# An mLSTM layer with a channel-mixing FFN: products with the old state summed in the bank of those within the chunk, PSUM as three rings, weight decoding without a clamp, and a new list

## The chip, the cores and the metric

The program runs on one core of one Trainium2 chip. TensorE (PE), VectorE (DVE), ScalarE (ACT) and GpSimd (POOL) each work through their own queue in the order in which the program was written for them; SyncE (SP) issues the transfers. The metric is device microseconds of one execution, as the median of several.

## The reference

Four batches of eight heads go through 768 steps of an mLSTM cell with a head size of 40; the result, seen as tokens of 320 numbers, goes through a channel-mixing feed-forward layer (FFN).

```python
for t in range(S):
    m_new = np.maximum(f_gate[:, :, t] + m, i_gate[:, :, t])
    f_stab = np.exp(f_gate[:, :, t] + m - m_new)
    i_stab = np.exp(i_gate[:, :, t] - m_new)
    m = m_new
    C = f_stab * C + i_stab * outer(vt, kt)
    n = f_stab * n + i_stab * kt
    h_tilde = C @ qt
    denom = np.maximum(np.abs(n @ qt), 1.0)
    y[:, :, t] = sigmoid(o_gate[:, :, t]) * h_tilde / denom
...
xk = mu_k * x + (1.0 - mu_k) * x_prev
xr = mu_r * x + (1.0 - mu_r) * x_prev
k = np.maximum(xk @ w_k, 0.0)
v = k * k @ w_v
r = sigmoid(xr @ w_r)
out = r * v
```

## The kernel before

The 768 steps are cut into six chunks of 128, and a **unit** is one chunk of two batches (NB = 2): units 0 and 1 are chunk 0 of batches 0, 1 and 2, 3, units 2 and 3 are chunk 1, and so on to unit 11. Each piece of work is a small function named with its unit `u` and the batch `i` within it; the body of the program is a list of calls of these functions, written out by hand (`load_w("wk", 0, SY)`, `ffn_k(0, 0)`, ...), and each engine gets its instructions in the order of that list. Nothing reorders them later.

*Attention of a unit.* `fetch_m` broadcasts the row of stabilisers of a batch to all partitions (tile `e`), `mask` (POOL) writes -1e30 where the key comes after the query, `exps` (ACT, eight of 128x128) makes the decay weights in place. In chunk 0 there is no row in DRAM yet: there `spread` makes it on PE, by eight products with a column of the identity (tile `pM`, K = 32), and `mask` clears the wrong half after `exps`. `scores` makes eight products of keys and queries (`pS`, two banks), `weigh` (DVE) multiplies them into `e`. `attend` does three things on PE: `e` times the values (`pI`, 16 products), the queries times the old state `C` (`pX`, eight), and the chunk's own addition to the state (`pX`, eight). In chunk 0 the second part is absent. `inter_v` (L306, DVE) scales the second part by the queries' decay `gk`, `total` (L314, DVE) adds the first, and `norm`, `gate`, `outcome`, `twin` make the layer's output `x`, which `turn` (PE) and `turned` (ACT) transpose. `carry_in` makes the scaled keys `kt`, `carry_old` the decayed state `Cd`, `carry_add` the new state.

*FFN of a unit.* `change` and `mix` (DVE, L373) make the mixed inputs, `mix_h` and `mix_l` (L388) split them in a high and a low part, so that PE can multiply in its fast format: `ffn_k` (L452, 16 products of 256 columns, four calls a unit, `pk`), `relu`, `square`, `square_h`, `square_l` (L479), `ffn_v` (L508, six products of 320 columns in a call, eight calls a unit, `pv`), `ffn_r` (L486, `pr`), `logits`, `sigmoid`, `result`, `store`.

*Weights.* They come as 64-bit floats, whose words the core turns into 32-bit floats, piece by piece: eight pieces of `wk` (384 wide), three of `wr` and eight of `wv` (320 wide). For each, `load_w` fetches, `size` (ACT, absolute value of the high word), `guard` (DVE, L413, a maximum with a smallest number), `bits` 0 to 2 (DVE, L420, L422, L424, shifts and masks), `parts` (the high part, mostly ACT) and `parts_l` (L436, the low part). This goes on beside units 0 and 1, so DVE has a great deal to do at the start.

*PSUM.* Eight banks: two for `pk` and the second `pr`, two for `pS`, two shared by `pI`, `pX` and the second `pv`, one for transposes and one for the first `pv` and the first `pr`.

*Fillers.* `warm(n)` issues n products of 512 columns of ones on PE (tile `pW`, L96), 58 in all, between the products of units 0 and 1.

What the prediction speaks of: `ffn_k(1, ·)`, the FFN of unit 1, before which PE has the whole of the start; `mix_l(0, "k")` and `mix_l(1, "k")`, the last DVE steps before `ffn_k(0, ·)` and `ffn_k(1, ·)`.

Of the kernel before, what the change touches and what calls it, by code (L numbers as in the profile page):

```python
# [18 lines left out]
P = 128  # L19
# [20 lines left out]
def mlstm_cmix_kernel(ctx: ExitStack, tc, kq, vk, og, gi, gf, wk, wr, wv, mu, pad, out):  # L40
# [8 lines left out]
    def bank(tag, name):  # L49
        return ps.tile([P, 512], F32, tag=tag, name=name, bufs=2 if tag in "kSA" else 1)  # L50
# [52 lines left out]
    gk = cp.tile([P, CPB, 2, BH], F32, name="gk")  # L103
# [106 lines left out]
    def mask(u, i):  # L210
# [55 lines left out]
    def attend(u, i):  # L266
# [3 lines left out]
        pI = t["I", i] = bank("A", "pI")  # L270
        pX = t["X", i] = bank("A", "pX") if cc else pI
        t["hv", i] = pI[:, :H * E1].rearrange("p (h x) -> p h x", x=E1)
        for h in range(H):
            at = slice(h * E1, (h + 1) * E1)
            for r in (slice(0, 64), slice(64, 128)):
                T.matmul(pI[r, at], t["e", i][:, h, r], t["va"][:, i, at], start=True, stop=True)  # L276
        if cc:
            for p in range(HH):
                at = slice(p * 2 * E1, (p + 1) * 2 * E1)
                for j in range(2):  # L280
                    s = i * L + 64 * j
                    T.matmul(pX[64 * j:64 * j + 64, at], kq_sb[u % 2][:KX, 1, p, s:s + 64], C[b][:KX, p, :],  # L282
                             start=True, stop=True)
        if cc < CPB - 1:
            for p in range(HH):
                for j in range(2):
                    h = p + HH * j
                    T.matmul(pX[64 * j:64 * j + D, H * E1 + p * E1:H * E1 + (p + 1) * E1], t["kt", i][:, h, :],  # L288
                             t["va"][:, i, h * E1:(h + 1) * E1], start=True, stop=True)

    def carry_add(u, i):
# [3 lines left out]
        pC = t["X", i][:, H * E1:H * E1 + HH * E1].rearrange("p (h x) -> p h x", x=E1)  # L295
# [6 lines left out]

    def inter_v(u, i):
        t, _, cc, _, bh = where(u, i)
        t1 = t["t1", i] = p2.tile([P, H, E1], F32, name="t1")
        V.tensor_tensor(t1.rearrange("p (j h) x -> p h j x", j=2),  # L306
                        t["X", i][:, :H * E1].rearrange("p (h j x) -> p h j x", j=2, x=E1),
                        gk[:, cc, 0, bh].rearrange("p (j h) -> p h j", j=2).unsqueeze(3)
                        .broadcast_to([P, HH, 2, E1]), op=ALU.mult)

    def total(u, i):
        t = units[u]
        t1 = t["t1", i]
        V.tensor_tensor(t1, t["hv", i], t1, op=ALU.add)  # L314
        t["hv", i] = t1
# [30 lines left out]
    def turn(u, i):  # L346
# [3 lines left out]
        pT = t["T", i] = bank(BANK["T"], "pT")  # L350
# [54 lines left out]
    def size(nm, i):  # L405
        p = pieces[nm, i]
        wf = p["wf"] = p2.tile([P, p["w"]], F32, tag="wf", name="wf", bufs=3)
        A.activation(wf, p["hi"].bitcast(F32), AF.Abs)

    def guard(nm, i):  # L410

        wf = pieces[nm, i]["wf"]
        V.tensor_scalar(wf, wf, SMALL, None, op0=ALU.max)  # L413

    def bits(nm, i, step):
# [3 lines left out]
        if step == 0:  # L419
            V.tensor_scalar(wb, wb, 3, 0x3FFFFFFF, op0=ALU.logical_shift_left, op1=ALU.bitwise_and)  # L420
# [1453 lines left out]
```

## Time and profile before

| | |
|---|---|
| median of 3 runs | 339.14 us (338.86 to 339.79) |
| span of the profiled execution | 336.5 us |
| its own time | not listed apart; the median of the runs lies 2.6 us above the span |
| PE busy | 321.8 us (96%) |
| DVE / ACT / POOL busy | 265.8 / 220.5 / 133.3 us |
| DMA | 41.99 MB |

The span goes from the first to the last instruction; the time has what lies around it too. Busy times of PE are modelled per product, so that they show where PE had something to do, not how fast. In the profile a product in full 32-bit format is recorded as two, so that eight calls of `scores` read x16.

### The profile page before, as it was taken

The page shows a single profiled execution, that of the slowest core. Times are in us where ns is not written, and L with a number is a line of the kernel's source. Part 1 is how long each engine was busy: PE and PEld are TensorE (multiplying, and loading weights), DVE is VectorE, ACT ScalarE, POOL GpSimd, SP SyncE. Part 2 cuts the span into 40 slices and gives each one's busy share as a digit, 9 for nine tenths or more (in the row PEclk, how much of TensorE's full clock was granted, in tenths as well). Part 3 has the DMA queues.
Part 4 walks back from the last instruction along what each step waited for, and adds up shares of the span by engine and source line. Part 5 has one row for each costly group of instructions (what it writes and reads, how often), then busy time and mean ns, then how long its engine had stood idle before and what let it go on. Part 6 is the DMA issues. An engine that isn't in the chain of part 4 may idle for free.

```text
span 336.5 us, 8857 instructions
## 1 busy us (share of the span) xinstructions
PE 321.8 (96%) x3544; PEld 296.7 (88%) x3548; DVE 265.8 (79%) x585; ACT 220.5 (66%) x484; POOL 133.3 (40%) x159
## 2 busy tenths in 40 slices
PE   8998895999999999999999999999999999999996
PEld 5576593999989999999999899999999899998995
DVE  6889999999999897767786976998596747778241
ACT  3577983689666768658828838839758655935350
POOL 2132234505333644455316435364524356353131
PEclk9979999699999999999999999999999999999999
DMA  6749644474523931612634641624214540010011
GB/s 207 248 144 288 177 171 160 126 215 152 152 103 97 285 106 34 209 64 86 157 98 131 215 124 51 228 84 143 59 64 109 193 163 0 5 58 2 0 42 39
DMA packets 14322, 41.99 MB, mean 125 GB/s; under 512 B 1912, under 2 KB 5144, under 8 KB 13320
## 3 DMA queue, kind: packets, MB, share of 16 engines
q1 hardware_dynamic: 14280, 41.41, 40.0%
q8 instruction: 28, 0.46, 0.6%
q14 instruction: 14, 0.11, 0.1%
HBM read 37.39 MB, written 4.01 MB: 123 GB/s over the span
## 4 chain that ended last, share of the span: by engine, by line
PE 70%; DVE 18%; ACT 6%; DMA 3%; issue 2%; POOL 0%; SPq 0%; ACTq 0%; POOLq 0%
PE pv L508 20%; PE pk L452 20%; PE pI L276 6%; PE pS L246 6%; PE pr L486 5%; PE pW L96 3%; PE pX L282 3%; PE pM L224 3%; ACT e L235 2%; DMA kq<-kq 2%; DVE e L251 2%; PE pT L352 2%; DVE kh L474 2%; DVE xm L373 1%; PE pX L288 1%
## 5 line engine op out<-in xcount | busy, mean ns | idle before, releaser
L452 PE MATMUL pk<-xlk,wkh 128*128 128x256 f32 x288 | 75.7, 279 | 0.0
L508 PE MATMUL pv<-wvh,kh 128*128 128x320 f32 x192 | 61.2, 319 | 0.2 <-DVE t L314 0.2
L508 PE MATMUL pv<-wvh,kl 128*128 128x320 f32 x192 | 59.3, 309 | 0.8 <-DVE kl L479 0.8
L508 PE MATMUL pv<-wvl,kh 128*128 128x320 f32 x192 | 59.2, 308 | 0.0
L458 ACT ACTIVATE rl<-pk 128x512 f32<-128x512 f32 x48 | 28.1, 590 | 42.4 <-PE pk L452 42.3
L452 PE MATMUL pk<-xhk,wkh 128*128 128x256 f32 x192 | 55.2, 287 | 0.0
L452 PEld LDWEIGHTS pk<-xlk,wkh 128*128 128x128 f32 x288 | 54.3, 188 | 0.0
L452 PE MATMUL pk<-xhk,wkl 128*128 128x256 f32 x192 | 53.5, 279 | 0.0
L235 ACT ACTIVATE e<-e,acol 128x128 f32<-128x128 f32 x160 | 50.0, 390 | 0.1
L214 POOL TENSOR_SCALAR_AFFINE_SELECT e<-e 128x1024 f32<-128x1024 f32 x24 | 28.0, 1166 | 47.0 <-DMA e<-nm 24.3
L479 POOL TENSOR_TENSOR kl<-kk,kh 128x512 fp32r<-128x512 f32 x20 | 28.7, 1436 | 39.4 <-DVE kh L474 25.7
L373 DVE SCALAR_TENSOR_TENSOR xm<-xd,mu_sb,xT 128x256 f32<-128x256 f32 x72 | 36.9, 567 | 3.1 <-POOL xd L367 3.0
L474 DVE CAST kh<-kk 128x512 fp32r<-128x512 f32 x44 | 24.4, 560 | 17.0 <-ACT kk L464 16.8
L452 PEld LDWEIGHTS pk<-xhk,wkh 128*128 128x128 f32 x192 | 36.2, 188 | 1.4 <-ACT rl L458 0.2
L508 PEld LDWEIGHTS pv<-wvh,kh 128*128 128x128 f32 x192 | 36.2, 188 | 1.0 <-issue 0.5
L508 PEld LDWEIGHTS pv<-wvh,kl 128*128 128x128 f32 x192 | 36.0, 188 | 1.0 <-DVE kl L479 1.0
L452 PEld LDWEIGHTS pk<-xhk,wkl 128*128 128x128 f32 x192 | 36.2, 189 | 0.0
L508 PEld LDWEIGHTS pv<-wvl,kh 128*128 128x128 f32 x192 | 36.1, 188 | 0.0
L251 DVE TENSOR_TENSOR e<-pS,e 128x512 f32<-128x512 f32 x48 | 32.1, 681 | 3.7 <-PE pS L246 3.2
L246 PE MATMUL pS<-kq 40*128 40x128 f32 x384 | 30.4, 293 | 1.0 <-DMA kq<-kq 1.0
L464 ACT ACTIVATE kk<-rl 128x512 f32<-128x512 f32 x48 | 29.5, 624 | 1.6 <-POOL kl L479 0.9
L276 PEld LDWEIGHTS pI<-vk_sb,e 128*64 128x64 f32 x768 | 24.8, 140 | 6.0 <-DVE e L251 1.9
(116 smaller groups left out, 724.6 us busy)
## 6 DMA issues: line engine op xcount, KB each, us to landing
e<-nm SPq DMA_DIRECT2D x20, 512.0 KB
vk_sb<-vk SPq DMA_DIRECT2D x12, 648.0 KB
kq<-kq SPq DMA_DIRECT2D x24, 320.0 KB
sg<-og SPq DMA_DIRECT2D x12, 320.0 KB
out<-sg SPq DMA_DIRECT2D x24, 160.0 KB
wst<-wk SPq DMA_DIRECT2D x8, 384.0 KB
wst<-wv SPq DMA_DIRECT2D x8, 320.0 KB
wst<-wr SPq DMA_DIRECT2D x3, 320.0 KB
```

The costliest lines, as they stand in the source:

```text
L214: G.affine_select(e, e, pattern=[[0, H], [1, L]], compare_op=ALU.is_ge, fill=NEG if cc else 0.0, base=0, channel_multiplier=-1)
L235: A.activation(e[:, h, :], src, AF.Exp, bias=acol[:, cc, b * H + h:b * H + h + 1])
L246: T.matmul(pS[j][:, p * L:(p + 1) * L], kq2[rw, 0, p, cs], kq2[rw, 1, p, cs], start=True, stop=True)
L251: V.tensor_tensor(ev, t["S", i, half], ev, op=ALU.mult)
L276: T.matmul(pI[r, at], t["e", i][:, h, r], t["va"][:, i, at], start=True, stop=True)
L373: V.scalar_tensor_tensor(xm[:, ct, :].rearrange("p (b t) -> p b t", b=NB), t["xd"][:, ct], mu_sb[:, "kr".index(nm), ct:ct + 1], xT[u % G2] ...
L452: T.matmul(pk[:, i * U:(i + 1) * U], ww[:, 2 * pr + i, ct * P:(ct + 1) * P], xx[:, ct, :], start=n == 0, stop=n == len(tl) - 1)
L458: A.activation(r, t["pk", pr], AF.Relu)
L464: A.activation(kk, t["r", pr], AF.Square)
L474: eng.tensor_copy(kh, t["kk", pr])
L479: eng.tensor_tensor(kl, t["kk", pr], t["kh", pr].bitcast(F32), op=ALU.subtract)
L508: T.matmul(t["pv", i][:, :DM], xx[:, ts], ww[:, f, :], start=f == 0 and n == 0, stop=f == NF - 1 and n == 2)
```

## The change

Four things change together.

1. The queries are scaled by their decay before the product with the old state. `gain` (ACT) makes exp of a whole row of 128 steps for all 32 heads and SP stores it in DRAM (`eg`, five times); `fetch_g` brings it back for each batch, broadcast over 64 partitions (two transfers, 64 x 4 x 128 each), and `queries` (DVE, 104x512) multiplies the queries into it. The product of these with the old state is then summed by PE in the same bank as `pI`. `inter_v` and `total` go, `pX` goes, and `columns` transposes two rows in place of three.
2. In chunk 0 the mask comes from PE: one product of 512 columns in each of `spread`'s eight banks (identity times a matrix of 0 and -1e30), on which the others are added. The four `mask` calls of chunk 0 go. Heads of a pair are neighbours now (2p and 2p + 1), so `exps` and `weigh` take every other head.
3. PSUM becomes three rings: two banks for `pI` and transposes, four for `pM`, `pS`, `pk` and `pr`, two for `pv`.
4. Weights are decoded without `guard`: `size` scales by a power of two, so `bits` 0 is one shift. The list of calls is made anew, with 12 fillers in place of 58. Ten `outcome`, ten `square_l` and three `mix_l` move from POOL to DVE, five `parts_l` of `wk` from DVE to POOL.

```diff
-SMALL = struct.unpack("<f", struct.pack("<I", (1023 - 127) << 20))[0]
-BANK = {"g": "T", "T": "T", ("r", 0): "v", ("r", 1): "k", ("v", 0): "v", ("v", 1): "A"}
+TO_SINGLE = 2.0 ** -112
+BANK = {"g": "A", "T": "A", "M": "B", "S": "B", "I": "A", "k": "B", ("r", 0): "B", ("r", 1): "B", ("v", 0): "v", ("v", 1): "v", "W": "v"}
+BANKS = {"A": 2, "B": 4, "v": 2}
...
+    def gain(c, eng):
+        eg = p2.tile([BH, L], F32, name="eg")
+        A.activation(eg, rows[c]["ar"][:, 1, :], AF.Exp)
+        eng.dma_start(eg_dram[c], eg)
...
     def spread(u, i):
...
+            T.matmul(pM, ident_b, later.unsqueeze(1).broadcast_to([P, HH, L]), start=True, stop=False)
...
+    def fetch_g(u, i, eng):
+        t, b, cc, _, bh = where(u, i)
+        t["g", i] = p2.tile([P, HH, L], F32, name="g")
+        rows_g = eg_dram[cc][bh, :].rearrange("(p j) t -> j p t", j=2)
+        for j in range(2):
+            eng.dma_start(t["g", i][64 * j:64 * j + 64], rows_g[j].partition_broadcast(64))
+
+    def queries(u, i, eng):
+        t, _, _, cs, _ = where(u, i)
+        q = t["g", i][:KX]
+        eng.tensor_tensor(q, kq_sb[u % 2][:KX, 1, :, cs], q, op=ALU.mult)
...
     def attend(u, i):
-        pI = t["I", i] = bank("A", "pI")
-        pX = t["X", i] = bank("A", "pX") if cc else pI
+        pI = t["I", i] = bank("I", "pI")
...
+                    mms.append((pI[r, at], t["g", i][:KX, p, r], C[b][:KX, p, :]))
...
+        for n, m in enumerate(mms):
+            T.matmul(*m, start=n < 2, stop=n >= len(mms) - 2, skip_group_check=True)
...
-    def inter_v(u, i):
...
-    def total(u, i):
...
     def size(nm, i):
-        A.activation(wf, p["hi"].bitcast(F32), AF.Abs)
-
-    def guard(nm, i):
-        wf = pieces[nm, i]["wf"]
-        V.tensor_scalar(wf, wf, SMALL, None, op0=ALU.max)
+        A.activation(wf, p["hi"].bitcast(F32), AF.Abs, scale=TO_SINGLE)
...
-            V.tensor_scalar(wb, wb, 3, 0x3FFFFFFF, op0=ALU.logical_shift_left, op1=ALU.bitwise_and)
+            V.tensor_scalar(wb, wb, 3, None, op0=ALU.logical_shift_left)
```

On PE, at the first attention (unit 0, both batches), the rows stood like this before: `attend(0, 0)`, `spread(1, 1)`, `attend(0, 1)`, fillers.

```order
L276 MATMUL pI<-vk_sb,e 64x41 x16
L288 MATMUL pI<-vk_sb,kt 40x41 x8
L224 MATMUL pM<-ar,ident 128x128 x8
L276 MATMUL pI<-vk_sb,e 64x41 x16
L288 MATMUL pI<-vk_sb,kt 40x41 x8
L96 LDWEIGHTS fill
L96 MATMUL pW<-fill 128x512
```

After the change the same place reads so (`scores(0, 1)`, `spread(1, 0)` with its two mask products, `attend(0, 0)`, `attend(0, 1)`):

```order
L268 MATMUL pS<-kq_75 128x128 x8
L229 LDWEIGHTS ident_b
L229 MATMUL pM<-later,ident_b 128x512
L232 MATMUL pM<-ar,ident 128x128 x4
L229 LDWEIGHTS ident_b
L229 MATMUL pM<-later,ident_b 128x512
L232 MATMUL pM<-ar,ident 128x128 x4
L313 MATMUL pI<-vk_sb,e 64x41 x16
L313 MATMUL pI<-vk_sb,kt 40x41 x8
L313 MATMUL pI<-vk_sb,e 64x41 x16
L313 MATMUL pI<-vk_sb,kt 40x41 x8
```

No filler stands between the fourth filler at the very start and the eight ahead of `ffn_k(0, 0)` any more, and the two `attend` follow each other.

On DVE, around the low part of unit 1's mixed input (`xlk`, which `ffn_k(1, ·)` waits for), the rows before were these; pieces of `wv` (tiles `wst`, `wf`, `wvl`) are decoded after it.

```order
L388 TENSOR_TENSOR xlk<-xm,xhk 128x768
L115 SCALAR_TENSOR_TENSOR bm<-ones,gf_sb 32x128
L424 SCALAR_TENSOR_TENSOR wf<-wst,wf 128x320
L123 SCALAR_TENSOR_TENSOR bm<-gf_sb,bm 32x128
L413 TENSOR_SCALAR wf<-wf 128x320
L422 SCALAR_TENSOR_TENSOR wf<-wst,wf 128x320
```

After the change the last piece of `wv` is decoded ahead of `xlk`:

```order
L425 TENSOR_SCALAR wf<-wf 128x320
L427 SCALAR_TENSOR_TENSOR wf<-wst,wf 128x320
L429 SCALAR_TENSOR_TENSOR wf<-wst,wf 128x320
L377 TENSOR_TENSOR xd<-xT_82 128x3x128 x2
L383 SCALAR_TENSOR_TENSOR xm<-xd,mu_sb,xT_82 128x256 x3
L273 TENSOR_TENSOR e<-pS,e 128x4x128
L441 TENSOR_TENSOR wvl<-wf,wvh 128x320
L398 TENSOR_TENSOR xlk<-xm,xhk 128x768
```

So all weights are decoded before the FFN of unit 1 begins, and PE does all eight `ffn_v(0, ·)` and `attend(2, 0)` ahead of `ffn_k(1, ·)`, where before it did them later. That last `attend` shows what else moved on PE; before, its second and third part went to a bank of their own:

```order
L276 MATMUL pI<-vk_sb,e 64x41 x16
L282 MATMUL pX<-C_75,kq_73 64x82 x8
L288 MATMUL pX<-vk_sb,kt 40x41 x8
```

After, all three go to one bank, and the second reads the scaled queries `g`:

```order
L313 MATMUL pI<-vk_sb,e 64x41 x16
L313 MATMUL pI<-C_77,g 64x82 x8
L313 MATMUL pI<-vk_sb,kt 40x41 x8
```

The number and shape of these products are the same.

## Rows read from the trace of the kernel before

**Rows 1.** The page: busy time, share of the span, instructions.

```profile
PE 321.8 (96%) x3544; PEld 296.7 (88%) x3548; DVE 265.8 (79%) x585; ACT 220.5 (66%) x484; POOL 133.3 (40%) x159
```

**Rows 2.** Windows: stretch, its length, busy PE, PEld, DVE, ACT, POOL, clock, DMA share, GB/s.

```profile
0.00:5.40 5.40, 3.88 (x12) 1.39 (x12) 2.60 (x9) 1.69 (x2) 1.83 (x12) 1.00 0.60 193
20.90:24.30 3.40, 3.40 (x32) 1.79 (x28) 3.40 (x8) 2.00 (x6) 0.38 (x1) 0.52 0.25 60
24.30:44.30 20.00, 17.09 (x276) 12.66 (x276) 19.24 (x53) 16.46 (x36) 5.42 (x8) 1.00 0.74 219
58.40:65.30 6.90, 6.89 (x32) 5.97 (x32) 6.90 (x13) 4.76 (x10) 4.40 (x4) 0.52 0.58 178
65.30:333.30 268.00, 264.79 (x3043) 255.47 (x3041) 206.20 (x445) 177.40 (x382) 111.98 (x127) 1.00 0.36 108
```

**Rows 3.** Timeline of PE, 0 to 66 us: start, length, line, products, idle before.

```profile
1.52 3.59 PE L96 MATMUL pW<-fill 128*128 128x512 bf16 x8 [1.52 <-DVE fill L70]
5.05 0.52 PE L156 MATMUL pt_g<-ident,ar 32*128 32x32 f32 x3
5.39 3.76 PE L224 MATMUL pM<-ar,ident 32*128 32x128 f32 x16
9.08 5.72 PE L96 MATMUL pW<-fill 128*128 128x512 bf16 x14
14.73 2.04 PE L224 MATMUL pM<-ar,ident 32*128 32x128 f32 x16
39.39 1.04 PE L96 MATMUL pW<-fill 128*128 128x512 bf16 x4
56.91 0.74 PE L352 MATMUL pT<-ident,x 128*128 128x128 f32 x3 [3.59 <-DVE x L340]
58.44 2.75 PE L246 MATMUL pS<-kq 40*128 40x128 f32 x16
65.87 0.28 PE L452 MATMUL pk<-xhk,wkh 128*128 128x256 f32 x1
```

**Rows 4.** Timeline of DVE, 0 to 80 us.

```profile
41.68 1.34 DVE L388 TENSOR_TENSOR xlk<-xm,xhk 128x768 fp32r<-128x768 f32 x1
66.27 0.29 DVE L413 TENSOR_SCALAR wf<-wf 128x320 f32<-128x320 f32 x1
77.95 0.49 DVE L436 TENSOR_TENSOR wvl<-wf,wvh 128x320 fp32r<-128x320 f32 x1
```

**Rows 5.** The chain that ended last, 104 to 116 us: start, length, work.

```profile
104.59 1.06 PE pI L276 x32
105.65 0.59 PE pX L282 x16
106.25 0.31 PE pX L288 x16
106.55 1.09 PE pS L246 x16
114.19 0.88 PE pv L508 x6
```

**Rows 6.** Groups by line and form: busy, mean ns of one, idle before.

```profile
L413 DVE TENSOR_SCALAR wf<-wf 128x384 f32<-128x384 f32 x8 | 3.3, 419 | 0.5 <-ACT wf L408 0.5
L413 DVE TENSOR_SCALAR wf<-wf 128x320 f32<-128x320 f32 x11 | 3.4, 312 | 0.0
L420 DVE TENSOR_SCALAR wf<-wf 128x320 int32<-128x320 int32 x11 | 6.6, 611 | 0.0
L306 DVE TENSOR_TENSOR t<-pX,gk 128x328 f32<-128x328 f32 x20 | 9.9, 496 | 17.0 <-PE pX L288 9.7 <-PE pX L282 7.3
L314 DVE TENSOR_TENSOR t<-pI,t 128x328 f32<-128x328 f32 x20 | 9.9, 493 | 0.3
L479 DVE TENSOR_TENSOR kl<-kk,kh 128x512 fp32r<-128x512 f32 x28 | 23.0, 822 | 0.3
```

**Rows 7.** The chain that ended last, 0 to 70 us: one transfer.

```profile
30.79 5.66 DMA kq<-kq
```

More of the change, by code (lines that the diff above doesn't have):

```diff
@@ L808, in mlstm_cmix_kernel @@
[L808 to L830 removed]
+    bits("wk", 7, 2)
@@ new lines, in mlstm_cmix_kernel @@
+    gate_o(5, SY)
+    mask(5, 1)
+    exps(5, 1, 1)
+    relu(3, 2)
+    norm(4, 1, 0)
+    norm(4, 1, 1)
+    norm(4, 1, 2)
+    gate(4, 1, V)
+    outcome(4, 1, V)
+    square(3, 2, A)
+    square_h(3, 2, V)
+    relu(3, 3)
+    scores(5, 0)
+    exps(5, 0, 1)
+    weigh(5, 0, 1)
+    turned(4, 0)
+    queries(5, 0, V)
+    exps(5, 1, 0)
+    scores(5, 1)
+    twin(4, 1, G)
+    square(3, 3, A)
+    square_h(3, 3, V)
+    turn(4, 1)
+    change(4, 0, V)
+    ffn_v(3, 1, 0, 1)
+    ffn_v(3, 1, 1, 2)
@@ new lines, in mlstm_cmix_kernel @@
+    carry_in(6, 0, V)
+    norm(5, 1, 0)
+    norm(5, 1, 1)
+    norm(5, 1, 2)
+    gate(5, 1, V)
+    outcome(5, 1, V)
+    carry_in(6, 1, G)
+    relu(4, 0)
+    square(4, 0, A)
+    square_h(4, 0, V)
+    fetch_g(6, 0, SY)
+    change(5, 0, V)
+    square(4, 1, A)
+    square_l(4, 0, V)
+    twin(5, 1, V)
+    square_h(4, 1, V)
+    square_l(4, 1, V)
+    ffn_k(4, 2)
+    relu(4, 2)
+    ffn_k(4, 3)
+    turn(5, 1)
+    exps(6, 0, 1)
+    ffn_v(4, 1, 0, 1)
+    ffn_v(4, 1, 1, 2)
+    load_o(6, SY)
@@ L1294, in mlstm_cmix_kernel @@
-    mix_l(5, "r", G)
-    norm(6, 0, 0)
-    norm(6, 1, 2)
-    load_o(7, SY)
-    norm(6, 0, 1)
-    columns(4)
-    relu(5, 3)
+    ffn_v(4, 0, 2, 3)
+    ffn_k(5, 1)
+    exps(6, 1, 1)
+    weigh(6, 1, 1)
+    sigmoid(4)
+    gate(6, 0, V)
+    attend(6, 1)
+    outcome(6, 0, V)
+    twin(6, 0, V)
+    carry_add(6, 0)
+    store(3, 0, SY)
+    scores(7, 0)
+    norm(6, 1, 0)
+    norm(6, 1, 1)
+    norm(6, 1, 2)
+    load_s(8, SY)
+    mix_h(5, "r")
+    square_l(4, 3, V)
+    relu(5, 0)
+    mix_l(5, "r", G)
@@ L1365, in mlstm_cmix_kernel @@
     norm(7, 0, 2)
+    square(6, 2, A)
+    gate(7, 0, V)
+    outcome(7, 0, V)
+    fetch_m(8, 1, SY)
+    mask(8, 1)
+    fetch_g(8, 0, SY)
+    ffn_v(5, 0, 2, 3)
+    mix_h(6, "r")
+    queries(8, 0, V)
+    ffn_v(5, 1, 3, 4)
+    result(5, 1)
+    ffn_k(6, 1)
+    relu(6, 1)
+    carry_in(7, 1, V)
+    twin(7, 0, V)
+    mix_l(6, "r", V)
+    turn(7, 0)
+    turned(7, 0)
+    store(4, 0, SY)
+    square_h(6, 2, V)
+    square_l(6, 2, G)
+    fetch_g(7, 1, SY)
+    queries(7, 1, V)
+    ffn_k(6, 0)
@@ new lines, in mlstm_cmix_kernel @@
+    sigmoid(6)
+    norm(8, 0, 2)
+    gate(8, 0, V)
+    queries(8, 1, V)
+    ffn_v(6, 0, 3, 4)
+    fetch_g(9, 1, SY)
+    queries(9, 1, V)
+    mix_h(7, "k")
+    carry_old(8, 1, V)
+    outcome(8, 0, V)
+    ffn_v(6, 1, 3, 4)
+    attend(8, 1)
+    carry_in(9, 0, G)
+    carry_old(8, 0, V)
+    fetch_m(9, 1, SY)
+    store(5, 1, SY)
+    mix_h(7, "r")
+    fetch_g(9, 0, SY)
+    carry_add(8, 0)
+    exps(9, 0, 0)
+    weigh(9, 0, 0)
+    carry_add(8, 1)
+    mix_l(7, "k", G)
+    ffn_k(7, 1)
```

2175 lines of the change are left out of this document (1007 added, 1168 removed).

## The prediction

> **What bounds the kernel now.** The page comes first: PE is busy for 321.8 of 336.5 us [rows 1], so it seems to bind throughout. That share is an average over two stages, and a table of windows parts them. From 65.3 to 333.3 us PE is idle for 268.0 - 264.8 = 3.2 us [rows 2]: there only PE counts. Before that its busy time says little, because fillers stand in it; the timeline of PE shows them in between the real products, and a gap of 3.59 us in front of one transpose, released by DVE [rows 3]. In the same stage DVE is busy for 19.24 of 20.0 us (24.3 to 44.3) and for all of 58.4 to 65.3 [rows 2]: it decodes weights. So the kernel is a start that ends with the first product of `ffn_k(1, ·)` at 65.87 [rows 3], set by DVE with PE and ACT in a chain, and a long stage set by PE. The question for each edit is which of the two it touches.
>
> The third thing is the clock. The windows show 0.52 from 20.9 to 24.3 and from 58.4 to 65.3 [rows 2]: the lower level, 1.2 of 2.4 GHz. They show 1.00 for 0 to 5.4, yet a filler takes 3.59 / 8 = 449 ns there and 5.72 / 14 = 409 ns from 9.08 on, against 1.04 / 4 = 260 ns at 39.39; `spread` takes 3.76 us at 5.39 and 2.04 at 14.73 [rows 3]. I therefore read the first 14 us as the lower level too, whatever that column says: lengths of equal work are the better witness. What PE did before 20.9 was `spread` and `scores`, narrow products of 32 and 40 rows; before 58.4 it had stood idle for 3.59 us.
>
> **The change part by part.**
>
> *The two DVE operations on the old state.* `inter_v` and `total` cost 9.9 + 9.9 us in 20 instructions each; `queries` adds 20 of 104x512. The nearest row is `square_l` on DVE, also two SBUF inputs and 512 columns, at 822 ns: 16.4 us, and below it the two removed ones, about 500 ns for 328 columns, give 20 x 0.50 = 10 us [rows 6]. With ten `square_l`, ten `outcome` and three `mix_l` more, DVE ends up with more work, not less. All but a first one or two lie after 65.9, beside a PE with 3.2 us of idle [rows 2]. If they wait on nothing late this is worth between -3.2 us (all of PE's idle recovered) and about +1.5 (a new stall in unit 1, where DVE barely keeps up); I take 0. The products keep number and shape; the new bank moves them without changing their 1.06 + 0.59 + 0.31 us [rows 5].
>
> The Trainium skill, "SBUF — State Buffer", section "Who interferes with whom", says that a DVE instruction with two SBUF inputs contends with a GpSimd one that reads SBUF; `queries` is such a one where `total` read PSUM. By that rule `queries` would lie at the dear end. The row agrees so far that `square_l` takes 822 ns where a 328-wide operation takes 493.
>
> *`guard`.* 19 instructions, 3.3 + 3.4 = 6.7 us of DVE [rows 6], all before 78.4. This one does lie in the start, where DVE sets the time; it is inside the counts below.
>
> *The start, step by step.* The gate transposes end and `spread` begins at 5.4 as now [rows 3]. The new list has four fillers, then `spread`, `spread`, `scores`, `columns`, `scores`, `spread`, `attend`, `attend`, all narrow, and no filler among them; I assume the lower level for all of it. Prices at that level: `spread` 3.76 plus two mask products of 512 columns at a filler's 0.45, 4.66; `scores` 2.75; `columns` 0.52 [rows 3]; `attend` of chunk 0, which no row shows alone at that level, twice 1.06 + 0.31 from the upper level [rows 5], 2.74. So 5.4 + 2 x 4.66 = 14.7; + 2.75 = 17.5; + 0.5 = 18.0; + 2.75 = 20.7; + 4.66 = 25.4; + 2 x 2.74 = 30.9, the end of `attend(0, 1)`. DVE does decoding in between, so it idles at first and is behind later. From the first `norm(0, 1)`, which waits for that, to `mix_l(0, "k")` the new order has 27 DVE instructions.
>
> Their price: from the end of `mix_l(0, "k")`, 41.68 + 1.34 = 43.0, to the end of the last decoded piece, 77.95 + 0.49 = 78.4, DVE now does 79 instructions [rows 4]: 35.4 / 79 = 0.448 us each. By parts: the 31 from 66.27 on take 12.2 us, 0.393 each; the 48 before take 23.3, 0.485, and there POOL is busy 4.40 of 6.9 us beside it [rows 2] and a shift of 128x320 takes 611 ns where `guard` of that size takes 312 [rows 6]. 27 x 0.448 = 12.1, so `mix_l(0, "k")` ends at 30.9 + 12.1 = 43.0, as now. From there to `mix_l(1, "k")` the new order has 74 instructions (fewer guards, but all decoding ahead of it): 74 x 0.448 = 33.2 (29.1 to 35.9), ending at 76.2. One `ffn_v(0, ·)` call, 0.88 [rows 5], still lies between it and `ffn_k(1, ·)`: 77.1.
>
> This is not a loss of 77.1 - 65.9, since PE will have done more by then: eight `ffn_v(0, ·)`, 8 x 0.88 = 7.04, and `attend(2, 0)`, 1.06 + 0.59 + 0.31 = 1.96 [rows 5]; 9.0 together. The point where nothing is won or lost is 65.9 + 9.0 = 74.9. At 77.1 the start costs 2.2 us. The fillers taken out cost nothing in the sum: they stand where PE would wait. What they cover is the clock, and that is priced above, at its lower level.
>
> *Sum.* Span 336.5 + 2.2 + 0 = 338.7; the median of the runs lies 339.14 - 336.5 = 2.6 above the span, so 341.3 us.
>
> **Rivals.**
>
> *A, the forecast:* 341.3, and by the two prices of a DVE instruction (101 of them) 341.3 - 5.6 = 335.7 to 341.3 + 3.7 = 345.0.
>
> *B, faster: the clock rises at once.* PE has work without a break from 5.4 on, and if that is enough, `spread` costs 2.04 + 2 x 0.26 = 2.56 and `scores` 1.09 [rows 3, 5]. Then the first scores are there at 5.4 + 5.1 + 1.1 = 11.6, half a us of exponents behind it, and DVE, with 46 instructions from there to `mix_l(0, "k")`, is the bound: 12.1 + 20.6 = 32.7, 10.3 us early; 66.8 at `ffn_k(1, ·)`, 8.1 below the point of no change: 331.0. It decides once `mix_l(0, "k")` ends before 40.8. Against it: PE was as busy from 1.5 to 14.7 and yet at the lower level [rows 3]. For it: the upper level did come by 14.73, with wide fillers before it.
>
> The Trainium skill, "TensorE: Matmul & The Clock Gate", Part 1, "What's actually happening", has it that the throttled state is the default and that activity releases it. Read plainly that is rival B, with its 331.0 us; the trace agrees only that the start is throttled and is released after a stretch of wide products.
>
> *C: the lower level lasts to the FFN.* After 30.9 come `spread(1, 1)` 4.66, two transposes 2 x 0.74, two `scores` 2 x 2.75, `attend(1, 0)` 2.74: 45.3; then a `norm` and `mix_l` 0.4 + 1.3 make 47.0, 4.0 late: 345.3. The filler rows at 39.39, 260 ns, speak for an upper level by then, but they have fillers ahead of them.
>
> *D: the rows of the decay arrive late.* `fetch_g` has to wait for a buffer that the attention two before it frees. The shortest cover is between two attentions of a unit: two `scores` and eight `ffn_v`, 2 x 1.09 + 8 x 0.88 = 9.2 us [rows 5]. A transfer on the chain landed after 5.66 [rows 7]; with `queries` behind it 6.5. It decides where landing takes over 8.4; 3 us late in three units would be 350. SP issues these transfers behind others, so a slow landing is not excluded.
>
> *E: the start as in A, but PE's 3.2 us of idle vanish:* 338.1.
>
> **How the numbers follow.** A 0.45, B 0.25, C 0.18, D 0.05, E 0.07. Of 339.14, 0.3% is 1.0 us, about what a measurement of this kernel can tell from no change. Faster (under 338.1): B's 0.25, the cheap end of A 0.10, a part of E 0.03: 0.38. The same (338.1 to 340.2): 0.14. Slower: the rest, 0.48. The likeliest case alone is 335.7 to 345.0; B just below and C just above widen it: 332 to 347 leaves out half of B, D and a little besides, about 0.2.
>
> **What the profile after would show.** Right: `spread` near 4.7 us in the first 15 us and `scores` near 2.75 until 20; the end of the second `attend` near 31; `mix_l(0, "k")` ending near 43 and the first product of `ffn_k(1, ·)` at about 77, with about 3 us of PE idle after it. DVE idles before its first product with the scores (after 17.5) and before its first `norm`. Wrong by B: `spread` near 2.6 from the second one on and `ffn_k(1, ·)` at 67. By C: `scores(1, ·)` still at 2.75. By D: idle of DVE ahead of `queries` put down to a DMA, and PE waiting behind it. Also wrong if DVE's instructions cost other than 0.39 to 0.49 us on average, because POOL now decodes more pieces beside them or because the masks of chunk 0 are off POOL.

## The result and the profile after

The changed kernel takes 342.33 us (median of 8 runs, 340.3 to 343.29) against 339.0 us of the kernel before (8 runs): a ratio of 1.0101, with a 95% interval of 1.0067 to 1.0136. It is slower by 1.0%, about 3.4 us; the forecast was 341.3 us, 2.2 us more than before. The profiled execution has a span of 340.4 us, 3.9 more than before. The number came out partly by luck: as the rest shows, the start was 4.2 us dearer than forecast and the long stage 2.5 us cheaper.

The timeline of PE shows the start (start, length, line, products; a product in full 32-bit format is recorded twice):

```profile
4.98 0.61 PE L229 MATMUL pM<-later,ident_b 128*128 128x512 bf16 x1
5.52 2.07 PE L232 MATMUL pM<-ar,ident 32*128 32x128 f32 x8
7.52 0.61 PE L229 MATMUL pM<-later,ident_b 128*128 128x512 bf16 x1
...
15.14 2.08 PE L268 MATMUL pS<-kq 40*128 40x128 f32 x16
...
29.00 0.68 PE L313 MATMUL pI<-vk_sb,kt 128*40 128x41 f32 x16
29.61 0.39 PE L229 MATMUL pM<-later,ident_b 128*128 128x512 bf16 x1
29.93 1.15 PE L232 MATMUL pM<-ar,ident 32*128 32x128 f32 x8
...
36.95 2.08 PE L268 MATMUL pS<-kq 40*128 40x128 f32 x16
...
79.00 0.64 PE L513 MATMUL pv<-wvl,kh 128*128 128x320 f32 x1 [2.80 <-DVE wvl L441]
...
81.30 0.41 PE L457 MATMUL pk<-xhk,wkh 128*128 128x256 f32 x1
```

The four products of `spread` in one bank take 2.07 us until 25 and 1.15 behind 29.9: the lower level, then the upper. Two `spread` fill 4.98 to 15.14, 5.08 us each. The second `attend` ends at 29.00 + 0.68 = 29.7. The first product of `ffn_k(1, ·)` starts at 81.30, where [rows 3] had 65.87. Ahead of it PE waits 2.80 us, and the products behind that wait take 0.41 to 0.64 us: the lower level again. The table of windows (columns as in [rows 2]) gives it in one line each:

```profile
5.00:15.10 10.10, 10.10 (x37) 7.50 (x36) 8.18 (x20) 5.83 (x19) 2.67 (x2) 1.00 0.76 237
32.50:41.40 8.90, 8.14 (x87) 6.94 (x88) 8.60 (x17) 4.35 (x11) 3.56 (x6) 0.52 0.73 228
79.00:81.30 2.30, 2.30 (x9) 2.30 (x9) 2.27 (x5) 2.27 (x3) 0.00 (x0) 0.50 0.00 0
81.30:337.20 255.90, 253.22 (x2923) 246.23 (x2922) 193.58 (x424) 170.40 (x364) 85.66 (x95) 0.99 0.43 121
```

The clock column says 1.00 for 5 to 15 us, in which the products take nearly twice their later length; as ahead of the prediction, the lengths are the witness there. The long stage (last line) has 2.7 us of PE idle, and DVE is busy for 76% of it, as before (206.2 of 268.0 in [rows 2], 77%).

On DVE, the timeline around the low part of both mixed inputs (`xlk`):

```profile
41.90 0.95 DVE L398 TENSOR_TENSOR xlk<-xm,xhk 128x768 fp32r<-128x768 f32 x1
...
65.24 0.33 DVE L425 TENSOR_SCALAR wf<-wf 128x320 int32<-128x320 int32 x1 [1.24 <-ACT wf L418]
...
74.76 3.06 DVE L383 SCALAR_TENSOR_TENSOR xm<-xd,mu_sb,xT 128x256 f32<-128x256 f32 x3
...
78.46 0.48 DVE L441 TENSOR_TENSOR wvl<-wf,wvh 128x320 fp32r<-128x320 f32 x1
78.86 0.95 DVE L398 TENSOR_TENSOR xlk<-xm,xhk 128x768 fp32r<-128x768 f32 x1
```

and of POOL beside the second one:

```profile
74.37 1.07 POOL L441 TENSOR_TENSOR wvl<-wf,wvh 128x320 fp32r<-128x320 f32 x1 [11.26 <-ACT wvh L435]
75.40 0.91 POOL L286 TENSOR_TENSOR Cd<-C,dec 128x328 f32<-128x328 f32 x1
76.27 1.27 POOL L221 TENSOR_SCALAR_AFFINE_SELECT e<-e 128x1024 f32<-128x1024 f32 x1
```

`mix_l(0, "k")` ends at 42.85 (forecast 43.0). `mix_l(1, "k")` ends at 79.81 (forecast 76.2). Near the end of this stretch, while POOL is busy without a gap from 74.37 to 77.54, three `xm` steps take 3.06 us. What PE waits for until 79.00 is not `mix_l` but the step before it, the low part of the last piece of `wv` (`wvl`, ending at 78.94); eight `ffn_v` products at the lower level follow and fill the time up to 81.30, and `xlk` is there by then.

The start is therefore 81.3 - 74.9 = 6.4 us behind the point of no change, not 2.2, and the long stage gives 2.5 back: from `ffn_k(1, ·)` to the end of the span there are 340.4 - 81.3 = 259.1 us, where before there were 336.5 - 65.9 = 270.6, less the 9.0 us of work that PE now does earlier, 261.6.

### The profile page after: what moved, and what is told of

It reads as the page before. It is cut to its first block, busy times and chain, and to the rows that moved or that the text cites. A ratio compares the mean times of both kernels' runs of the same rounds, so it can differ in the third digit from the quotient of the medians.

```text
span 340.4 us, 8826 instructions
## 1 busy us (share of the span) xinstructions
PE 323.1 (95%) x3504; PEld 303.4 (89%) x3504; DVE 263.2 (77%) x576; ACT 223.3 (66%) x488; POOL 105.5 (31%) x129
## 4 chain that ended last, share of the span: by engine, by line
PE 54%; DVE 19%; DMA 7%; ACT 4%; issue 2%; SPq 1%; DVEq 0%; ACTq 0%
PE pk L457 18%; PE pv L513 17%; PE pI L313 7%; PE pr L491 6%; PE pS L268 4%; DVE xm L383 4%; DMA vk_sb<-vk 3%; DMA g<-eg 3%; DVE e L273 2%; PE pT L362 1%; DMA wst<-wv 1%; DVE g L246 1%; DVE wf L429 1%; DVE x L354 1%; DVE wf L427 1%
## 5 line engine op out<-in xcount | busy, mean ns | idle before, releaser
L457 PE MATMUL pk<-xlk,wkh 128*128 128x256 f32 x288 | 76.5, 282 | 0.6 <-DVE xlk L398 0.6
L513 PE MATMUL pv<-wvl,kh 128*128 128x320 f32 x192 | 60.2, 313 | 3.7 <-DVE wvl L441 2.8
L513 PE MATMUL pv<-wvh,kl 128*128 128x320 f32 x192 | 60.3, 314 | 0.3 <-DVE kl L484 0.2
L457 PEld LDWEIGHTS pk<-xlk,wkh 128*128 128x128 f32 x288 | 55.0, 191 | 1.0 <-DVE xlk L398 1.0
L457 PEld LDWEIGHTS pk<-xhk,wkh 128*128 128x128 f32 x192 | 36.9, 192 | 0.3
L221 POOL TENSOR_SCALAR_AFFINE_SELECT e<-e 128x1024 f32<-128x1024 f32 x20 | 25.5, 1277 | 34.9 <-DMA e<-nm 34.8
L479 DVE CAST kh<-kk 128x512 fp32r<-128x512 f32 x44 | 21.1, 483 | 16.9 <-ACT kk L469 16.8
L469 ACT ACTIVATE kk<-rl 128x512 f32<-128x512 f32 x48 | 29.7, 628 | 1.7 <-DVE kl L484 0.5
L313 PE MATMUL pI<-vk_sb,e 128*64 128x41 f32 x768 | 29.6, 241 | 0.5 <-DVE e L273 0.5
L313 PEld LDWEIGHTS pI<-vk_sb,e 128*64 128x64 f32 x768 | 26.8, 149 | 3.3 <-issue 1.2
```

The lines of the kernel that those rows point to most:

```text
L313: T.matmul(*m, start=n < 2, stop=n >= len(mms) - 2, skip_group_check=True)
L457: T.matmul(pk[:, i * U:(i + 1) * U], ww[:, 2 * pr + i, ct * P:(ct + 1) * P], xx[:, ct, :], start=n == 0, stop=n == len(tl) - 1)
L469: A.activation(kk, t["r", pr], AF.Square)
L479: eng.tensor_copy(kh, t["kk", pr])
L513: T.matmul(t["pv", i][:, :DM], xx[:, ts], ww[:, f, :], start=f == 0 and n == 0, stop=f == NF - 1 and n == 2)
```

## Experiments

The ratios below are all against the kernel before; the changed kernel itself stands at 1.0101. Times of different rounds differ by up to 0.5% for the same kernel, so ratios are compared, not times.

**POOL taken out of the way.**

```diff
     parts("wv", 6, A)
-    parts_l("wv", 6, G)
...
     change(1, 1, V)
+    parts_l("wv", 6, V)
...
     mix_l(1, "k", V)
-    carry_old(2, 0, G)
...
-    mask(3, 0)
...
+    carry_old(2, 0, G)
+    mask(3, 0)
     ffn_k(1, 3)
```

> Three POOL steps are taken out of the stretch in which DVE makes the mixed input of unit 1: the low part of the piece wv 6 goes to DVE (about 0.5 us there), and carry_old(2, 0) and mask(3, 0) are written behind mix_l(1, k). Theory 1 (the start is late because DVE's instructions with two SBUF inputs are stretched beside POOL): the three xm steps at 74.8 take about 1.3 us in place of 3.06, the first product of ffn_k(1, .) comes 1 to 2 us before 81.3, and the time falls by 1 to 4 us below the 342.3 of the changed kernel (the larger figure if PE's wait gets so short that its clock stays at the upper level). Rival (the stretch is paid for by transfers of weights and by ACT, DVE's lengths only fill the time): ffn_k(1, .) stays at 81 and the time within 1 us of 342.3.

Ratio 1.0053 (1.0024 to 1.0081), 0.5% under the changed kernel. The timelines of DVE and PE of this run:

```profile
75.10 1.27 DVE L383 SCALAR_TENSOR_TENSOR xm<-xd,mu_sb,xT 128x256 f32<-128x256 f32 x3
```

```profile
77.54 0.59 PE L513 MATMUL pv<-wvl,kh 128*128 128x320 f32 x1 [1.61 <-DVE wvl L441]
...
79.80 0.41 PE L457 MATMUL pk<-xhk,wkh 128*128 128x256 f32 x1
```

POOL's two other steps were written behind `mix_l(1, "k")` but ran earlier, from 63.2 to 65.4, since POOL no longer waited for the piece of `wv`; from there until past 81 POOL did nothing. The same three steps take 1.27 us without POOL beside them: 1.79 us of their 3.06 was the stretch. `ffn_k(1, ·)` comes 1.5 us earlier. Theory 1 holds, near the lower end of what it gave. It bears out the rule of the Trainium skill ("SBUF — State Buffer", "Who interferes with whom") that the prediction weighed: a DVE instruction with two SBUF inputs contends with a GpSimd one that reads SBUF.

**Fillers that hold the clock ahead of `ffn_k(1, ·)`.**

```diff
+    def keep(u, i, n):
+        for _ in range(n):
+            T.matmul(units[u]["pv", i][:, 320:512], fill, fill.unsqueeze(1).broadcast_to([P, 2, P])[:, :, :96],
+                     start=False, stop=False, skip_group_check=True)
...
+    keep(0, 1, 32)
     ffn_v(0, 0, 3, 4)
```

> 32 products of 192 columns into unused columns of pv(0, 1), ahead of ffn_v(0, 0, 3, 4), where PE of the changed kernel waits from 75.9 to 79.0 and then works at the lower level until 83.2. Theory (the clock that falls in that wait costs time, since only PE counts from there on): the products from 79.0 on run at the upper level, 4.2 us of work at half speed become 2.1, the time falls by about 2 us below 342.3. Rival (the clock falls anyway, or DVE is the bound behind that place): no change, or up to 1 us more if the fillers end after the wait.

Ratio 1.0072 (1.0039 to 1.0105). The timeline of PE:

```profile
30.22 2.07 PE L232 MATMUL pM<-ar,ident 32*128 32x128 f32 x8
...
75.52 2.81 PE L518 MATMUL pv<-fill 128*128 128x192 bf16 x32
...
80.28 0.42 PE L513 MATMUL pv<-wvl,kh 128*128 128x320 f32 x1 [1.33 <-DVE wvl L441]
...
81.68 0.28 PE L457 MATMUL pk<-xlk,wkh 128*128 128x256 f32 x1
```

The products behind the wait run at the upper level (0.28 us in place of 0.41): the mechanism is as expected. The size is not settled, since 0.3% lies within both intervals, and in the profiled execution DVE came 1.3 us later to this place. The reason lies earlier, where the two kernels issue the same products: here `spread(1, 1)` was still at the lower level (2.07 us for four products at 30.22), where the changed kernel had 1.15 at 29.93. So a single execution can put `ffn_k(1, ·)` off by over a microsecond, with the clock as the only difference found.

**No mask in chunk 0.**

```diff
-            T.matmul(pM, ident_b, later.unsqueeze(1).broadcast_to([P, HH, L]), start=True, stop=False)
...
-                         start=False, stop=h == HH - 1)
+                         start=True, stop=True)
```

> Leaves out the mask of chunk 0 altogether (the eight products with the matrix of 0 and -1e30 in spread), so those keys that come after a query are counted there. Theory (PE's narrow products at the lower level set the first 30 us): each of the eight took 0.54 us, six of them lie ahead of the end of attend(0, 1), which comes 3.2 us before 29.6; DVE waited 6.4 us for PE ahead of it, so mix_l(0, k) ends 2 to 3 us before 42.85 and the time falls by 2 to 3 us. Rival (the weights' transfers and DVE's decoding set the time of ffn_k(1, .) anyway, as the chain after shows from 61.9 on): ffn_k(1, .) moves by less than 1 us and so does the time.

Ratio 0.9969 (0.9941 to 0.9996): 1.3% under the changed kernel, and no slower than before. Its timelines, of PE and then of DVE:

```profile
4.99 7.17 PE L231 MATMUL pM<-ar,ident 32*128 32x128 f32 x32
...
16.87 3.77 PE L231 MATMUL pM<-ar,ident 32*128 32x128 f32 x16
...
24.56 0.76 PE L312 MATMUL pI<-vk_sb,kt 128*40 128x41 f32 x16
...
77.02 0.41 PE L456 MATMUL pk<-xhk,wkh 128*128 128x256 f32 x1
```

```profile
37.54 0.95 DVE L397 TENSOR_TENSOR xlk<-xm,xhk 128x768 fp32r<-128x768 f32 x1
```

The second `attend` ends 4.4 us earlier, `mix_l(0, "k")` 4.4, `ffn_k(1, ·)` 4.3. Only six of the eight mask products lie ahead of the second `attend`; at 0.54 us they would make 3.2. But the products around them became shorter as well: the three `spread` ahead of it take 7.17 + 3.77 = 10.9 us here and 3 x 5.08 = 15.2 in the changed kernel, so each mask product cost about 0.7 us in all. These 4.3 to 4.4 us lay on the path to their full length, though DVE does all the decoding beside it. The last two, in `spread(1, 1)`, added nothing that shows. The theory holds, and its size (2 to 3 us) was too small. This run does less work than either kernel, so it shows what the mask costs where it stands, not what another place for it would bring; the next run does that.

**The mask on POOL again.**

```diff
-            T.matmul(pM, ident_b, later.unsqueeze(1).broadcast_to([P, HH, L]), start=True, stop=False)
...
     exps(0, 1, 1)
+    mask(0, 1)
...
     exps(0, 0, 1)
+    mask(0, 0)
```

and the same for unit 1, with 0 as the fill of `mask` in chunk 0, as before.

> The changed kernel with one part undone: the mask of chunk 0 is made by POOL again, behind exps, and spread has no mask products. Theory (the eight products on PE at the lower level lengthen the chain that sets the start, as the run without any mask showed, 1.4% under the changed kernel): four POOL masks of about 1.2 us lie off that chain, so ffn_k(1, .) comes near 77 and the time is 1.0 to 1.4% under the changed kernel, 0.997 to 1.001 of the kernel before. Rival (POOL's masks stretch DVE's decoding beside them, or come late for weigh): half of it or less, 1.004 or more of the kernel before.

Ratio 1.0050 (1.0018 to 1.0081): the rival, half of it. The timelines of PE and then of DVE, whose first product with the scores waits for the mask and whose first `norm(0, 1)` waits for PE:

```profile
25.59 3.78 PE L231 MATMUL pM<-ar,ident 32*128 32x128 f32 x16
```

```profile
14.88 1.29 DVE L272 TENSOR_TENSOR e<-pS,e 128x512 f32<-128x512 f32 x2 [1.19 <-POOL e L221]
...
25.71 0.17 DVE L334 TENSOR_SCALAR den<-pI 128x8 f32<-128x8 f32 x1 [1.04 <-PE pI L312]
```

`ffn_k(1, ·)` starts at 78.86, 2.4 us before 81.30 and 1.8 behind the run without a mask. Not all of these 1.8 us need be POOL's: in this execution `spread(1, 1)` ran at the lower level (3.78 us), in the run without a mask at the upper (2.08 at 25.24). How much of the difference between the two ratios, 0.8%, is the mask on POOL and how much the clock is not shown.

**All three together** (the mask on POOL, POOL's three steps moved, 22 fillers for 32).

> The mask on POOL, the three POOL steps taken out of the way of the mixed input of unit 1, and 22 fillers ahead of ffn_v(0, 0, 3, 4), all on the changed kernel. If the three costs are apart, their gains add: 1.0 to 1.4% for the mask, 0.5% for the POOL steps, 0.3 to 0.6% for the clock, which is 0.985 to 0.992 of the kernel before. Rival (they are one wait seen three times): no better than the best alone, 0.996 or more.

Ratio 0.9984 (0.9952 to 1.0016). The three gains (0.51, 0.48 and 0.29%) make 0.9973 from 1.0101; that lies within the interval, so they add as far as can be told. The time itself is in the rival's range (0.996 or more), because the size named for the mask beforehand was too large; but it is 0.7% better than the best of the three alone, so they are not one wait seen three times. The changed kernel is then level with the one before.

**12 fillers put back between the two `spread` of unit 0.**

```diff
+    warm(12)
     spread(0, 0)
```

> The changed kernel with 12 fillers between the two spreads of unit 0, where the kernel before had 14. Theory A (wide products raise the clock, and that is what the fillers of before bought): they take about 5.2 us, the clock is at the upper level behind them, so spread(0, 0) takes 2.6 us in place of 5.1, scores 1.1 in place of 2.1, and about half or all of the 5.2 us is given back by the end of attend(0, 1), which comes between 29 and 32; the time stays within 0.5% of the changed kernel. Rival (the lower level holds whatever PE does in the first 28 us): attend(0, 1) ends near 34.8 and the time is about 1.3% over the changed kernel.

Ratio 1.0237 (1.0189 to 1.0284). PE's timeline:

```profile
9.95 5.30 PE L101 MATMUL pW<-fill 128*128 128x512 bf16 x12
...
15.40 1.15 PE L232 MATMUL pM<-ar,ident 32*128 32x128 f32 x8
...
20.11 2.08 PE L268 MATMUL pS<-kq 40*128 40x128 f32 x16
...
31.18 0.76 PE L313 MATMUL pI<-vk_sb,kt 128*40 128x41 f32 x16
...
83.93 0.41 PE L457 MATMUL pk<-xhk,wkh 128*128 128x256 f32 x1
```

The clock does rise behind the wide fillers (`spread` 1.15) and is back at the lower level at 20, with PE busy all the while (`scores` 2.08). Of 5.3 us of fillers, 31.9 - 29.7 = 2.2 are left at the end of `attend(0, 1)` and 2.6 at `ffn_k(1, ·)`. So the mechanism of theory A is seen, and its end of `attend(0, 1)` (29 to 32) too; its balance is not: the time, 1.3% over the changed kernel, is that of the rival.

**The kernel before with the new decoding alone** (no `guard`, the scale and the shift as in the diff of the change, and the mask of `bits` 1 that goes with them).

> The kernel before with nothing but the new decoding: size scales, bits 0 is one shift, the 19 guards are gone, the list otherwise as before. Theory (DVE's decoding sets the start): 6.7 us of DVE are gone, about 5.5 of them ahead of the FFN of unit 1, so ffn_k(1, .) comes 3 to 5.5 us before 65.9 and the time is 3 to 5.5 us under the kernel before. Rival (ahead of ffn_k(1, .) it is PE, ffn_r at the lower level, or the waits for ACT and for transfers, that sets the time): less than 1.5 us gained.

Ratio 0.9940 (0.9912 to 0.9968), about 2 us. Waits of DVE, 0 to 66 us (us in total, times, longest), of this run and, below, of the kernel before:

```profile
DVE den L325 <- PE pI L288: 2.7, 3, 1.3
```

```profile
DVE den L325 <- PE pI L288: 0.6, 1, 0.6
```

DVE now waits where it worked, 2.1 us more in front of `den` alone, and `ffn_k(1, ·)` starts at 65.55 for 65.87. Most of the 5.5 us that this removes ahead of it became waiting. The gain lies between the theory (3 to 5.5 us) and the rival (under 1.5), nearer the rival. Only 0.3 us of it shows at `ffn_k(1, ·)`, and the span of this execution is 1.2 us shorter; where the rest comes from is not shown.

**The same and 8 more fillers ahead of `turn(1, 1)`.**

```diff
+    warm(8)
     turn(1, 1)
```

> The kernel before with the new decoding (no guards) and 8 more fillers ahead of the transpose turn(1, 1), where PE waited for DVE from 54 to 56.5 and worked at the lower level from 58.1 to 65.0 behind that. Theory (the clock that falls in this wait is what holds ffn_k(1, .) at 65.5 when the guards are gone): scores and ffn_r run at the upper level, ffn_k(1, .) comes near 63.3, and the time is 2 us under the run with the new decoding alone, 0.985 to 0.990 of the kernel before. Rival (DVE sets ffn_k(1, .) also there, or the fillers delay the transpose): 0.993 or more.

Ratio 0.9963 (0.9933 to 0.9993): no better than without the fillers. The clock held, PE was at `ffn_k(1, ·)` at 63.22, and then stood, as its timeline shows:

```profile
63.22 0.38 PE L452 MATMUL pk<-xhk,wkh 128*128 128x256 f32 x1
64.70 0.39 PE L452 MATMUL pk<-xlk,wkh 128*128 128x256 f32 x1 [1.10 <-DVE xlk L388]
```

DVE sets that place too, as the rival had it.

**The kernel before with 12 fillers for 58** (the first four and the last eight ahead of `ffn_k(0, 0)`).

> The kernel before with 12 fillers in place of 58: the first four and the last eight ahead of ffn_k(0, 0). Theory (fillers stand where PE would wait, and they hold the clock up): the narrow products of the first 40 us run at the lower level, spread 4.1 us and scores 2.1 in place of 2.0 and 1.1 from 14.7 on, but 5.7 us of fillers go, so attend(0, 1) ends within 2 us of 28.7, DVE stays the bound, and the time is within 0.5% of the kernel before. Rival (fillers cost PE time on the path): the time falls by over 0.5%. Other rival (the lower level costs more than the fillers did): it rises by over 0.5%.

Ratio 1.0136 (1.0089 to 1.0184). Its PE:

```profile
9.82 3.78 PE L224 MATMUL pM<-ar,ident 32*128 32x128 f32 x16 [1.10 <-ACT e L235]
13.53 2.08 PE L246 MATMUL pS<-kq 40*128 40x128 f32 x16
...
67.68 0.28 PE L452 MATMUL pk<-xhk,wkh 128*128 128x256 f32 x1
```

`spread` stays at 3.78 us where [rows 3] had 2.04, and `ffn_k(1, ·)` comes 1.8 us late: in that list the fillers bought more clock than they cost. The second rival holds.

**Queries twice.**

```diff
+        eng.tensor_tensor(q, kq_sb[u % 2][:KX, 1, :, cs], q, op=ALU.mult)
         eng.tensor_tensor(q, kq_sb[u % 2][:KX, 1, :, cs], q, op=ALU.mult)
```

> The changed kernel in which each of the 20 queries on DVE is done twice in place (so the queries themselves are multiplied in twice, and the output is another). 20 more DVE instructions of 0.68 us, 13.7 us. Theory (this work lies beside PE in the long stage, so its price is nothing but the first one, ahead of ffn_k(1, .)): 0 to 1.5 us more than the changed kernel, 1.008 to 1.015 of the kernel before. Rival (DVE is near enough to PE that its work is paid for): 4 us or more, over 1.02.

Ratio 1.0449 (1.0403 to 1.0494), 3.4% over the changed kernel, and a span of 349.9, 9.5 us more, of which 0.75 lies ahead of `ffn_k(1, ·)` (82.05). The theory falls. Windows of this run:

```profile
84.00:120.00 36.00, 34.56 (x353) 33.37 (x353) 30.17 (x67) 24.37 (x53) 8.90 (x13) 0.89 0.33 89
120.00:160.00 40.00, 38.29 (x463) 36.99 (x463) 37.03 (x76) 23.32 (x56) 17.34 (x19) 1.00 0.57 167
```

DVE is busy for 37.0 of 40 us in the second, where the changed kernel had 34.3, and PE is idle for 1.7 us, where it had 0.9; the clock falls once more in the first. DVE has little room in the long stage; its work there is hidden only as long as its amount stays what it was.

**FFN products by turns.** A helper issues the products of two neighbouring calls alternately, in 17 pairs:

```diff
-    ffn_v(2, 0, 3, 4)
...
-    ffn_k(3, 1)
+    by_turns((ffn_v, (2, 0, 3, 4)), (ffn_k, (3, 1)))
```

> The changed kernel with 17 pairs of neighbouring calls, ffn_v and ffn_k or ffn_r, whose products are issued by turns: PE changes between kinds of product 318 times in place of 148, with the same products and banks. Theory (the long stage of the changed kernel is about 3 us shorter than before because its order changes kind 122 times behind ffn_k(1, .) in place of 172; the first product behind a change takes about 0.05 us longer than the next): 170 more changes cost 6 to 10 us, 1.027 to 1.04 of the kernel before. Rival (the gain of the long stage comes from something else): within 1.5 us of the changed kernel, 1.006 to 1.015 of the kernel before.

Ratio 1.0116 (1.0079 to 1.0152): nothing lost by 170 more changes. The theory falls as it was put.

**Attention and FFN by turns**, the same helper on ten pairs of `attend` or `scores` and `ffn_v`.

> The changed kernel with ten pairs of neighbouring calls, one of attend or scores and one ffn_v, whose products are issued by turns: PE goes 55 times more from a product of the FFN to one of the attention and 55 times more back; products and banks are the same. The by-turns run among FFN products (170 more changes) cost nothing; the traces show the first FFN product behind an attention product at about 0.24 us, others at 0.14. Theory (a change between the two kinds costs about 0.1 us each way, and the changed kernel's long stage is shorter since it has 30 such round trips behind ffn_k(1, .) where the kernel before had 41): 5 to 11 us over the changed kernel, 1.025 to 1.043 of the kernel before. Rival (no change of kind costs time in itself, the first products only show a delay that the next ones make up): within 1.5 us of the changed kernel, 1.006 to 1.015.

Ratio 1.1191 (1.1114 to 1.1268), span 375.5, 35.1 us more than the changed kernel: the direction of the theory, far beyond its size. PE's timeline and a window:

```profile
158.21 0.41 PE L527 MATMUL pv<-wvl,kh 128*128 128x320 f32 x1
158.55 0.31 PE L527 MATMUL pI<-vk_sb,e 128*64 128x41 f32 x2
158.79 0.41 PE L527 MATMUL pv<-wvh,kl 128*128 128x320 f32 x1
```

```profile
132.00:138.00 6.00, 6.00 (x66) 5.57 (x66) 2.21 (x9) 1.79 (x3) 1.27 (x2) 0.50 0.44 124
```

From one `pv` to the next 0.58 us pass with one product of `attend` between them. Alone, a `pv` product takes 0.88 / 6 = 0.15 and one of `attend` 1.06 / 16 = 0.07 [rows 5], so the round trip costs about 0.37, and 55 of them 20 us. The rest is the clock: it is at the lower level four times behind 84 us in this run, in the window above with PE busy throughout. By the clock column these four last about 31 us together; at half speed that loses 15, and 20 + 15 is the 35 measured.

The same price can be read from the kernels before and after, where whole calls alternate at the upper level. In the changed kernel two `scores` and two `attend` stand in a row, ahead of a product of `ffn_v`:

```profile
244.16 2.06 PE L268 MATMUL pS<-kq 40*128 40x128 f32 x32
246.15 1.13 PE L313 MATMUL pI<-vk_sb,e 128*64 128x41 f32 x32
...
249.94 0.41 PE L513 MATMUL pv<-wvh,kh 128*128 128x320 f32 x1
```

From start to start, two `scores` take 1.99 us and two `attend` 3.79; alone, in the kernel before, they take 1.09 and 1.06 + 0.59 + 0.31 = 1.96 [rows 5]. Every block of `scores` thus costs 0.20 us and every block of `attend` 0.13 beside its calls. In the full timelines of both kernels the last FFN product ahead of such a block takes 0.09 us more than the others and the first one behind it 0.10 more: 0.32 us in all around an `attend`, 0.39 around a `scores`.

## Why the prediction came out, point by point

- *The lower level in the start*: right. `scores`, two `attend` and the end at 29.7 (forecast 30.9) were all at that level; `spread` was dearer (5.1 us for 4.66), `scores` (2.0 for 2.75) and `attend` (2.3 for 2.74) cheaper. That `mix_l(0, "k")` ended where forecast is two errors that cancel: `attend(0, 1)` ended 1.2 us early, and the 27 DVE instructions behind it, from the first `norm(0, 1)` at 29.73 on, took 42.85 - 29.73 = 13.1 us for 12.1. The experiments add what the walk didn't say: six mask products cost 4.4 us there, 1.3% of the time, as much as the whole loss and more. With the mask on POOL as before, half of the loss is left.
- *The price of a DVE instruction from there on, "74 x 0.448 = 33.2 (29.1 to 35.9)"*: this step failed. It took 79.81 - 42.85 = 37.0 us, 0.50 each, outside its bounds. The prediction named this beforehand as a sign of being wrong (other than 0.39 to 0.49 us, because of POOL). Two pieces stand out: 1.8 us is the stretch of three `xm` beside POOL, which moving POOL's steps away took back, and 1.24 a wait for ACT, behind a late piece of `wv`; without these two it would be 0.46 each. A mean of before carried the collisions of before, not those of the new list.
- *The last `ffn_v(0, ·)`, 0.88*: from `mix_l(1, "k")` to `ffn_k(1, ·)` it was 1.5. The path was another one than forecast: PE waited 2.8 us for the last `wvl`, was at the lower level behind that, and had eight `ffn_v` products left, 2.3 us of them.
- *The long stage, "I take 0"*: this failed too, by -2.5 us, or -3.8 if the 1.3 us lost to the clock from 81.3 to 83.8 is taken off. The sum said that the products keep number and shape, and left out in what order they come. PE changes less often between attention and FFN: in the traces of this stage `scores` stands in 11 blocks for 18, `attend` in 15 for 20 (four of them double), the FFN is entered from attention or `columns` 12 times for 21 and left for them 14 times for 21 (transposes of `x`, behind which it is entered 18 times for 20, not counted). At the prices read from the two traces above, that is 7 x 0.20 + 4 x 0.13 + 9 x 0.10 + 7 x 0.09 = 3.5 us, and PE's idle is 0.5 us less: together a little more than the 3.8. No run has only that difference, but the last one shows that such changes cost time.
- *`guard`*: costing it inside a count of DVE instructions was too simple. Alone it brings 0.6%; most of what it takes off DVE turns into waits for PE.
- *`queries` at 0, "beside PE"*: at 683 ns (median) they cost less than the 822 taken, and DVE's share of the long stage is the same as before, so no loss shows. But the reason given, that PE's idle is all there is to lose, does not hold: 20 more such instructions cost 9.5 us.
- *The fillers "cost nothing in the sum"*: right as it was put, with the clock priced apart; in the list of before, 12 for 58 cost 1.4%.
- *Rivals.* B, the clock rises at once: no; PE was busy from 5 to 25 us at the lower level. C: half. The level fell again from 32.5 to 41.4 (`scores` 2.08), but DVE was busy for 8.60 of these 8.90 us, and `mix_l(0, "k")` was not late. D: DVE waited for the rows of the decay once, 0.8 us. E: PE's idle in the long stage is 2.7 us for 3.2.

The errors of the second and third point (+3.8 and +0.6 us) and of the fourth (-2.5) partly cancelled, which is luck; 1.7 us is left, the 3.9 of the two spans for the 2.2 forecast. The range was wide enough for either side alone.

## What to carry to other kernels

Work moved onto an engine for its idle time has to be priced at the clock that this engine has at that place: six mask products at the lower level on the path cost 1.3%, and a freed POOL didn't pay for them. A mean price of an instruction is only as good as what runs beside it: look at which instructions of the neighbour will overlap the last ones ahead of the point that counts. And ask of "hidden" work how far the hiding engine is from full: DVE at 76% on average stood at over 90% in stretches once its load was raised, and it was paid for.

The best version here that does the whole work is the kernel before with the new decoding alone, 0.9940 (0.9912 to 0.9968); with 8 more fillers it can't be told from that (0.9963).

## What the runs showed of the hardware that was not expected

- `spread` and `scores` (products of 32 and 40 rows) held PE busy from 5 to 25 us and the clock stayed at the lower level, with and without the mask products between them. Behind 12 fillers of 512 columns it was at the upper one (`spread` 1.15 at 15.40), and under `spread` and `scores` at the lower again at 20.11. Fillers are not the only thing ahead of a rise: in the changed kernel and in the run without a mask the level rose right behind two `attend` (at 29.9 and 25.2), with the fillers ahead of `ffn_k(1, ·)` and with the mask on POOL it did not at the same place (`spread` 2.07 at 30.22, 3.78 at 25.59). The Trainium skill ("TensorE: Matmul & The Clock Gate", Part 1, "What's actually happening") speaks of activity that releases the throttle; these rows show that being busy in the profile's sense was not enough.
- In the last run the level fell with no idle time of PE, in or right behind stretches where attention and FFN products alternate (0.50 in the window from 132 to 138 us).
- A change between attention and FFN products and back costs about 0.37 us when single products alternate, and 0.3 to 0.4 around whole calls; one between two kinds of FFN products nothing that shows (1.0116 for 1.0101). The Trainium skill ("TensorEngine Tiling (Array Packing)", "Key Properties") states that changing the tiling mode drains TensorE; `attend` writes 64 rows at a time where the FFN writes 128, so this fits, but the two also differ in their number format, and no run here parts the two. One part of the price doesn't need the narrower writes: in the trace of the changed kernel an FFN block behind a transpose of `x`, which writes 128 rows as the FFN does, is longer by 0.09 us too (twelve `ffn_v` products 1.85 us for 1.76).
